# A new written order for the instructions of an attention and expert kernel, from chunk 1 to the end

## The chip, the cores and the metric

The kernel runs on one core of one Trainium2 chip. The core has five engines, each with its own queue of instructions: TensorE (PE, matmuls), VectorE (DVE), ScalarE (ACT), GpSimd (POOL) and SyncE (SP), which here only issues DMAs. The metric is device time in microseconds (us) for one launch.

## The reference

Attention over 8 batches, 8 heads, 576 positions of 64 columns, in two parts that are added: a full attention over q, k and v averaged by fours (144 positions, each result repeated four times), and a local one in which a position sees only those less than four away. The 4608 rows of 512 columns that come out go through a gated layer:

```
q_d = q.reshape(B, H, Sd, 4, D).mean(axis=3)        # k_d, v_d in the same way
out_up = np.repeat(sm_attn(q_d, k_d, v_d), 4, axis=2)
mask = np.abs(pos[:, None] - pos[None, :]) < 4
out_local = softmax(where(mask, scale * q @ k.T, -1e9)) @ v
x = (out_up + out_local).transpose(0, 2, 1, 3).reshape(4608, 512)
out = (np.maximum(x @ w_gate, 0) * (x @ w_val)) @ w_out   # 512 -> 1536 -> 512
```

Inputs and output are float32; matmul operands are fp16.

## The kernel before

**Tiling.** The rows are cut into 9 chunks of 512. The attention of a chunk is done by pairs of heads, four pairs to a chunk, two to each of its two units (`u` 0 and 1; pairs `a` and `b`). While the layer of chunk c is computed, the attention of the next rows and the output product of chunk c-1 are interleaved with it, so that PE always has a matmul.

**Seven products.** The gate layer (`Gate7`, L1295 to L1313: `sq` product, `sk` copy on ACT, `sf` finish on DVE or ACT) and the output layer (`Out7`, the same lines: `up`, `uk`, `uf`) replace eight block products by seven, at the price of fp16 sums of operand blocks. For the output these are sums of the gated activations `gT`, made on DVE by `Unit.sums` (L1030) in four steps of 768 columns, called `sum`, `sumhi` and `next`; the fourth writes the tile `s4`. The sums of x are `xq` (L1282). The value layer (`vh`, L951) is plain, and `gt` (L1390) multiplies gate and value on DVE.

**Attention steps.** `qk` and `v` load from POOL's queue (L468, L486), `v4` loads the v for averaging from SP's queue (L520, two pieces), `scores` computes scores and issues on SP the DMA transpose of q and k three pairs ahead (L529), `pool` averages q and k (L536, DVE), `v2` and `v1` average v by two additions on POOL (L573, L581), `mask` (L862), `xn` and `xsum` (L902, L906) are DVE steps. `after`, `tn` and `tm` are copies of one element on POOL into a tile `seen` (L1465, L1524): they make POOL, and through it whatever depends on POOL's position, wait until a tile has been read or written.

**The order.** Nothing plans the order: it is written out. `SEQ` is one string of 2338 steps, run from first to last under a manual schedule, so each engine gets its instructions in exactly the order in which the steps stand. Semaphore waits are added where data or a buffer demands them. A step such as `sq/4.0.0.1/0@3` says what, with which bank, and for unit 0 of chunk 3; `sq/4.0.2.1/0@3` is the same product with another tile. Steps that begin with `t:` belong to the last two chunks: `q`, `k`, `o` and `qv`, `kv`, `ov` are the layers, `p` (L1199), `s` (L1210) and `e` (L1215, L1217) product, copy and finish of the output, `y` an output DMA of 128 rows by 256 columns on SP. The finished rows lie in `y_sb`, a pool (`ypool`) of four buffers: a later unit's finish into a buffer waits until the DMA that reads it has landed.

The fp16 sums and the guard of `s4`:

```
def sums(self, lo=0, hi=NK, which=range(4)):
    ...
    for o, a, b, op in (ops[i] for i in which):
        nc.vector.tensor_tensor(
            out=o[:, lo:hi, :], in0=a[:, lo:hi, :], in1=b[:, lo:hi, :], op=op
        )
...
"after": lambda w, i: nc.gpsimd.tensor_copy(out=seen, in_=w.s4[:, NK - 1, 127:128]),
...
def emit_v2(hp):
    ...
        nc.gpsimd.tensor_tensor(out=m, in0=t[:, :, 0:128], in1=t[:, :, 128:256], op=ALU.add)
```

Of the kernel before, what the change touches and what calls it, by code (L numbers as in the profile page):

```python
# [42 lines left out]
ex/7/0/4 ma/7/0 hv/9/*/1 hg/9/*/0 relu/9/0 wt/0 hv/10/*/6 hg/10/*/3 relu/10/3 gate/9/1 gate/10/6 qk/a0/1@0
next/0/1@0 vd/7/4 qk/b0/1@0 qk/a1/1@0 hg/11/*/7 relu/11/7 next/1/1@0 flip/9 hv/11/*/0 p/1/0@1 gate/11/0 sumhi/0/0@1
v/a/1@0 vc/7/4 num/7/1/7 tr/8/0/1 keep/1/0@1 zero/b/6 ev/8/01A/1 wt/1 v/b/0@0 num/7/0/6 tr/8/1/0 wt/2 den/7/0/4
den/7/1/5 ln/4 sumhi/1/0@1 p/2/0@1 c11//0@1 zs/1.1/0@1 qk/b2/0@1 qk/b2/1@0 p/6/0@1 vd/8/5 ev/8/00A/1 inv xn/6
p/5/0@1 next/0/0@1 keep/2/0@1 vc/8/5 ev/8/10A/0 p/7/0@1 ev/8/11A/0 scores/a/0@1 exp/a1/0@1 xsum/7 keep/3/0@1
hg/0/0@1 qk/b3/1@0 hv/0/0@1 wt/3 relu/0/0@1 qk/a0/0@1 flip/10 qk/a2/0@1 mask/a1/0@1 hg/2/0@1 next/2/0@1 sum/3/0@1
ed/a/0@1 o/a11/0@1 c22//0@1 exp/a0/0@1 mask/a0/0@1 next/1/0@1 p/4/0@1 o/a01/0@1 qk/a3/0@1 zs/1.0/0@1 tn/1/0@1
gate/0/0@1 c21//0@1 o/a10/0@1 ln/a1/0@1 p/3/0@1 flip/11 next/3/0@1 qk/b3/0@1 c12//0@1 relu/2/0@1 qk/b1/0@1 o/a00/0@1  # L50
ln/a0/0@1 inv/a/0@1 pool/b/0@1 xn/a1/0@1 hg/1/0@1 relu/1/0@1 zero/b/1 v2/a/1@1 hg/4/0@1 zero/b/5 hv/1/0@1 gate/1/0@1
hv/2/0@1 xn/a0/0@1 qk/b0/0@1 vd/9/7 vc/9/7 hg/3/0@1 relu/3/0@1 flip/12 gate/2/0@1 xsum/a/0@1 zs/2.0/0@1 scores/b/0@1
exp/b0/0@1 mask/b0/0@1 exp/b1/0@1 mask/b1/0@1 qk/a3/1@1 hv/3/0@1 gate/3/0@1 vd/10/2 ed/b/0@1 zs/3.0/0@1 vc/10/2
v4/b/1@0 hv/4/0@1 relu/4/0@1 gate/4/0@1 pool/a/0@1 tn/3/0@1 o/b00/0@1 o/b01/0@1 ln/b0/0@1 v/b/1@0 o/b10/0@1
o/b11/0@1 ln/b1/0@1 p/1/1@1 inv/b/0@1 xn/b0/0@1 hg/5/0@1 keep/1/1@1 xn/b1/0@1 hv/5/0@1 p/2/1@1 c11//1@1 p/6/1@1
scores/a/1@1 flip/13 relu/5/0@1 hg/0/1@1 qk/a0/1@1 zero/b/2 p/5/1@1 xsum/b/0@1 qk/a1/1@1 exp/a0/1@1 keep/2/1@1
p/7/1@1 mask/a0/1@1 gate/5/0@1 exp/a1/1@1 mask/a1/1@1 ed/a/1@1 o/a00/1@1 relu/0/1@1 pool/b/1@1 qk/a2/1@1 qk/b0/1@1
keep/3/1@1 c22//1@1 zero/d/0 v/a/0@1 pool/a/1@1 v2/b/0@1 v4/b/0@1 v1/a/1@1 o/a01/1@1 ln/a0/1@1 o/a11/1@1 o/a10/1@1
v/b/0@2 hv/0/1@1 qk/b1/1@1 ln/a1/1@1 inv/a/1@1 const/2 qk/a3/0@2 xn/a0/1@1 p/4/1@1 c21//1@1 p/3/1@1 kk/a0/1@1
kk/a1/1@1 qk/b3/1@1 hg/2/1@1 relu/2/1@1 flip/14 hg/1/1@1 relu/1/1@1 xn/a1/1@1 qk/a1/0@2 scores/b/1@1 exp/b0/1@1  # L60
zero/v/1 qk/a2/0@2 hg/3/1@1 c12//1@1 hv/1/1@1 exp/b1/1@1 gate/0/1@1 qk/a0/0@2 hv/2/1@1 zs/2.1/0@1 zero/b/3 zero/v/0
mask/b1/1@1 tm/b/1@1 v/a/0@2 v4/a/1@1 ed/b/1@1 mask/b0/1@1 o/b00/1@1 o/b10/1@1 zs/3.1/0@1 zero/b/0 gate/1/1@1
zero/d/1 v1/b/1@1 v/a/1@1 o/b01/1@1 relu/3/1@1 ln/b0/1@1 gate/2/1@1 o/b11/1@1 zero/v/2 hv/3/1@1 gate/3/1@1 ln/b1/1@1
qk/b2/1@1 hg/4/1@1 hg/5/1@1 qk/b1/0@2 xsum/a/1@1 inv/b/1@1 xn/b1/1@1 v/b/0@1 xn/b0/1@1 kd/a1/1@1 v2/b/1@1 v4/b/1@1
qk/b0/0@2 hv/4/1@1 kd/a0/1@1 relu/5/1@1 relu/4/1@1 gate/4/1@1 hv/5/1@1 gate/5/1@1 zero/b/4 v/b/1@1 zero/k/1
qk/b3/0@2 qk/b2/0@2 xsum/b/1@1 up/2.1/0@2 xq/0/0@2 xq/1/0@2 kk/b0/0@2 sq/4.0.0.1/0@2 xq/2/0@2 scores/a/0@2
vh/10.6/0@2 uk/2.1/0@2 sk/4.0.0.1/0@2 sq/4.0.0.2/0@2 sq/4.0.0.5/0@2 sq/4.0.0.6/0@2 sumhi/0/0@2 kk/b1/0@2 vh/4.7/0@2
sf/4.0.0.11/0@2 xq/3/0@2 sk/4.0.0.2/0@2 v2/a/0@2 sq/4.0.0.3/0@2 next/0/1@1 sk/4.0.0.5/0@2 sq/4.0.0.7/0@2 up/2.5/0@2
sumhi/1/0@2 exp/a0/0@2 ed/a/0@2 next/1/1@1 kk/a1/0@2 sf/4.0.0.22/0@2 sq/4.0.0.4/0@2 sf/4.0.0.21/0@2 mask/a0/0@2
sf/4.0.0.12/0@2 gt/4.7.0/0@2 up/2.6/0@2 uk/2.2/0@2 uk/2.5/0@2 sq/0.0.2.1/0@2 sq/0.0.2.5/0@2 sk/0.0.2.5/0@2 sum/2/0@2  # L70
sum/3/0@2 gt/10.6.1/0@2 o/a00/0@2 o/a01/0@2 up/2.7/0@2 sk/0.0.2.1/0@2 uf/2.22/0@2 sq/0.0.2.6/0@2 sk/0.0.2.2/0@2
ln/a0/0@2 inv/a/0@2 pool/b/0@2 next/0/0@2 up/2.2/0@2 o/a10/0@2 sq/0.0.2.3/0@2 sq/0.0.2.2/0@2 sf/0.0.2.11/0@2
sq/0.0.2.7/0@2 v1/a/0@2 after/3/0@2 sf/0.0.2.22/0@2 sf/0.0.2.12/0@2 kd/b0/0@2 o/a11/0@2 xn/a0/0@2 up/2.4/0@2
kd/b1/0@2 up/2.3/0@2 uf/2.21/0@2 v2/b/0@2 uf/2.11/0@2 uf/2.12/0@2 sq/0.0.2.4/0@2 sf/0.0.2.21/0@2 pool/a/0@2
sq/1.1.0.1/0@2 sq/1.1.0.5/0@2 sk/1.1.0.5/0@2 scores/b/0@2 v4/b/0@2 vh/0.7/0@2 sk/1.1.0.1/0@2 sq/1.1.0.6/0@2 v1/b/0@2
exp/b0/0@2 gt/0.7.2/0@2 vh/6.3/0@2 gt/6.3.3/0@2 mask/b0/0@2 sk/1.1.0.2/0@2 kd/a0/0@2 sq/1.1.0.2/0@2 sq/1.1.0.7/0@2
sf/1.1.0.22/0@2 ed/b/0@2 kd/a1/0@2 sq/1.1.0.3/0@2 kk/a0/0@2 v4/a/0@2 vh/1.0/0@2 o/b00/0@2 sf/1.1.0.11/0@2 kk/b1/1@2
sq/1.1.0.4/0@2 sf/1.1.0.21/0@2 o/b01/0@2 sf/1.1.0.12/0@2 ln/b0/0@2 o/b10/0@2 sq/2.2.0.1/1@2 sq/2.2.0.5/1@2
vh/7.1/0@2 o/b11/0@2 xsum/a/0@2 sk/2.2.0.1/1@2 next/2/0@2 sq/2.2.0.6/1@2 sq/2.2.0.2/1@2 inv/b/0@2 scores/a/1@2
sk/2.2.0.5/1@2 gt/1.0.0/0@2 qk/a1/1@2 gt/7.1.1/0@2 xn/b0/0@2 sk/2.2.0.2/1@2 v1/a/1@2 up/0.1/1@2 tm/b/0@2 qk/b3/1@2  # L80
sq/2.2.0.7/1@2 v/a/1@2 ed/a/1@2 sq/2.2.0.3/1@2 sf/2.2.0.11/1@2 kk/a0/1@2 up/0.5/1@2 sf/2.2.0.22/1@2 sq/2.2.0.4/1@2
sf/2.2.0.21/1@2 next/1/0@2 v2/b/1@2 uk/0.1/1@2 sf/2.2.0.12/1@2 qk/a0/1@2 qk/a2/1@2 vh/8.7/1@2 pool/b/1@2 qk/a1/0@3
sq/3.2.1.1/1@2 up/0.6/1@2 gt/8.7.1/1@2 exp/a0/1@2 mask/a0/1@2 kd/b0/1@2 sq/3.2.1.5/1@2 vh/2.4/1@2 gt/2.4.0/1@2
sk/3.2.1.1/1@2 sq/3.2.1.2/1@2 sk/3.2.1.5/1@2 sq/3.2.1.6/1@2 uk/0.2/1@2 uk/0.5/1@2 qk/a3/1@2 xsum/b/0@2 o/a00/1@2
o/a11/1@2 sk/3.2.1.2/1@2 next/3/0@2 tm/a/1@2 up/0.7/1@2 uf/0.22/1@2 sf/3.2.1.11/1@2 o/a01/1@2 v/b/1@2 sq/3.2.1.3/1@2
sq/3.2.1.7/1@2 o/a10/1@2 sf/3.2.1.22/1@2 kk/b0/1@2 pool/a/1@2 kd/b1/1@2 ln/a0/1@2 sf/3.2.1.12/1@2 up/0.2/1@2
inv/a/1@2 xn/a0/1@2 sq/3.2.1.4/1@2 sf/3.2.1.21/1@2 scores/b/1@2 v/b/0@3 exp/b0/1@2 up/0.3/1@2 sq/5.2.0.1/1@2
ed/b/1@2 sq/5.2.0.5/1@2 sk/5.2.0.5/1@2 up/0.4/1@2 mask/b0/1@2 o/b00/1@2 xsum/a/1@2 sk/5.2.0.1/1@2 sq/5.2.0.6/1@2
uf/0.21/1@2 uf/0.11/1@2 uf/0.12/1@2 o/b01/1@2 vh/3.0/1@2 gt/3.0.1/1@2 tm/b/1@2 vh/9.1/1@2 gt/9.1.2/1@2
sk/5.2.0.2/1@2 v2/a/1@2 o/b10/1@2 sq/5.2.0.7/1@2 qk/b1/1@2 qk/b2/1@2 v1/b/1@2 qk/a0/0@3 sq/5.2.0.3/1@2 ln/b0/1@2  # L90
sq/5.2.0.2/1@2 o/b11/1@2 sf/5.2.0.22/1@2 qk/a2/0@3 vh/5.4/1@2 inv/b/1@2 v4/b/1@2 kd/a0/1@2 qk/b0/1@2 qk/b3/0@3
sf/5.2.0.12/1@2 xn/b0/1@2 qk/a3/0@3 sf/5.2.0.11/1@2 sq/5.2.0.4/1@2 qk/b0/0@3 v4/a/1@2 qk/b2/0@3 v/a/0@3
sf/5.2.0.21/1@2 gt/5.4.0/1@2 xsum/b/1@2 vh/11.1/1@2 gt/11.1.1/1@2 kk/a1/1@2 kd/a1/1@2 qk/b1/0@3 up/2.1/0@3 xq/0/0@3
xq/1/0@3 kk/b0/0@3 sq/4.0.0.1/0@3 xq/2/0@3 scores/a/0@3 vh/10.6/0@3 uk/2.1/0@3 sk/4.0.0.1/0@3 sq/4.0.0.2/0@3
sq/4.0.0.5/0@3 sq/4.0.0.6/0@3 sumhi/0/0@3 kk/b1/0@3 vh/4.7/0@3 sf/4.0.0.11/0@3 xq/3/0@3 sk/4.0.0.2/0@3 v2/a/0@3
sq/4.0.0.3/0@3 next/0/1@2 sk/4.0.0.5/0@3 sq/4.0.0.7/0@3 up/2.5/0@3 sumhi/1/0@3 exp/a0/0@3 ed/a/0@3 next/1/1@2
kk/a1/0@3 sf/4.0.0.22/0@3 sq/4.0.0.4/0@3 sf/4.0.0.21/0@3 mask/a0/0@3 sf/4.0.0.12/0@3 gt/4.7.0/0@3 up/2.6/0@3
# [1526 lines left out]
```

## Time and profile before

| what | value |
|---|---|
| time, median of 3 runs | 343.49 us (342.92 to 344.7) |
| the profiled execution | 343.54 us, span 341.8 us |
| clock granted to TensorE | 1.00 in every stretch |
| PE busy | 331.0 us, 97% of the span |
| DVE, ACT, POOL busy | 292.9, 272.1, 188.6 us |
| transfers | 43.91 MB, 128 GB/s in the mean |

The page gives for each engine its busy time, share and instructions; for a group of instructions its line, engine, operation, output and inputs, shapes, count, then busy time and the mean in ns; in square brackets or behind a bar the idle time just before and what ended it. A row of the timeline begins with its start and its length in us. A DMA row ends with the KB of one and the median us from issue to landing. The span is the recorded stretch; the execution's own time is 1.7 us longer. In the steady part, chunks 2 to 5, one chunk takes about 35 us.

### The profile page before, as it was taken

How to read it: one execution, taken by the hardware profiler on the slowest of the kernel's cores; microseconds unless marked ns; L12 is line 12 of the kernel's file. 1: busy time of each engine (PE TensorE's matmuls, PEld its weight loads, DVE VectorE, ACT ScalarE, POOL GpSimd, SP SyncE). 2: the span in 40 equal slices, each digit the busy share in tenths (PEclk: the TensorE clock that was granted, in tenths of full speed). 3: DMA queues.
4: the chain of work that ended last, by engine and by line, in shares of the span. 5: the costliest groups of instructions: out<-in, count | busy, mean ns of one | idle time of the engine just before them, and what ended most of it. 6: DMA issues, size and time to landing. Idle time of an engine off the chain costs nothing.

```text
span 341.8 us, 9062 instructions
## 1 busy us (share of the span) xinstructions
PE 331.0 (97%) x3410; PEld 243.5 (71%) x3410; DVE 292.9 (86%) x578; ACT 272.1 (80%) x653; POOL 188.6 (55%) x268
## 2 busy tenths in 40 slices
...
GB/s 135 165 170 208 185 194 167 150 186 148 168 187 133 192 88 218 128 185 105 220 118 194 92 191 151 189 122 190 51 33 1 63 2 93 3 15 109 3 56 130
DMA packets 162176, 43.91 MB, mean 128 GB/s; under 512 B 147500, under 2 KB 156820, under 8 KB 162132
## 3 DMA queue, kind: packets, MB, share of 16 engines
...
q10 hardware_dynamic: 112, 0.02, 0.0%
...
## 4 chain that ended last, share of the span: by engine, by line
PE 79%; DMA 6%; DVE 5%; POOL 4%; ACT 3%; issue 2%; DVEq 0%; ACTq 0%; POOLq 0%
PE ps L1295 24%; PE ps L951 24%; PE ps L1199 17%; DMA qk<-in_k_dram 3%; PE ps L1036 3%; DMA wv_sb<-in_moe_w_val_dram 3%; PE ps L867 2%; POOL qk L463 2%; PE ps L840 2%; PE ps L887 1%; PE ps L882 1%; POOL vw L513 1%; PE ps L836 1%; DVE xo L1030 1%; DVE xT L1175 1%
## 5 line engine op out<-in xcount | busy, mean ns | idle before, releaser
L951 PE MATMUL ps<-xT,wv_sb 128*128 128x512 f16 x352 | 89.4, 379 | 0.0
L951 PEld LDWEIGHTS <-wv_sb 128*128 128x128 f16 x352 | 32.5, 97 | 27.5
L468 POOL DMA_DIRECT2D qk<-in_k_dram x46 | 33.6, 732 | 19.3 <-DMA qkT<-qk 16.3
L1390 DVE SCALAR_TENSOR_TENSOR gT<-r,ps 128x512 f16<-128x512 f16 x55 | 37.5, 682 | 6.1 <-PE ps L951 5.1
L1295 PE MATMUL ps<-xT,qk 128*128 128x256 f16 x240 | 40.9, 272 | 0.0
L468 POOL DMA_DIRECT2D qk<-in_q_dram x46 | 34.0, 740 | 12.1 <-DMA qkT<-qk 7.1
L1306 ACT COPY ps<-ps 128x256 f32<-128x256 f32 x80 | 29.0, 366 | 8.1 <-PE ps L1295 7.4
L1295 PE MATMUL ps<-xT,wg_sb 128*128 128x256 f16 x180 | 33.9, 272 | 1.1 <-DVE xT L1313 0.6
L536 DVE TENSOR_REDUCE qkd<-qkT 128x288 f16<-128x1152 f16 x23 | 30.8, 1338 | 0.0
L486 POOL DMA_DIRECT2D vw<-in_v_dram x40 | 28.9, 732 | 2.3 <-DMA qk<-in_q_dram 1.7
L1311 ACT CAST r<-ps 128x256 f16<-128x256 f32 x55 | 20.2, 367 | 11.0 <-DVE r L1313 6.3
L581 POOL TENSOR_TENSOR vd<-v 48x192 f16<-48x192 f32 x40 | 26.0, 650 | 1.7
L1210 ACT COPY ps<-ps 128x256 f32<-128x256 f32 x54 | 19.4, 366 | 9.1 <-PE ps L1199 7.3
L951 PE MATMUL ps<-xT,wg_sb 128*128 128x512 f16 x104 | 26.1, 380 | 0.5 <-ACT r L960 0.5
L1295 PEld LDWEIGHTS <-qk 128*128 128x128 f16 x240 | 22.2, 97 | 4.8
L573 POOL TENSOR_TENSOR v<-v 112x384 f32<-112x384 f32 (+1 forms) x21 | 22.6, 1074 | 4.0 <-DMA v<-in_v_dram 3.6
L1295 PEld LDWEIGHTS <-xo 128*128 128x128 f16 x240 | 22.5, 97 | 2.9 <-DVE xo L1030 0.2
L1295 PEld LDWEIGHTS <-wg_sb 128*128 128x128 f16 x180 | 17.0, 97 | 10.7 <-issue 3.1
L1295 PE MATMUL ps<-wt,xo 128*128 128x256 f16 x180 | 24.5, 272 | 0.0
L920 ACT ACTIVATE rden<-rden 128x720 f32<-128x720 f32 x28 | 22.5, 803 | 0.8
L1313 DVE TENSOR_TENSOR r<-ps,xT 128x256 f16<-128x256 f32 x44 | 18.1, 418 | 4.4 <-PE ps L1295 3.1
L963 DVE TENSOR_TENSOR gT<-r,ps 128x512 f16<-128x512 f16 x24 | 16.1, 679 | 6.0 <-PE ps L951 3.2
...
## 6 DMA issues: line engine op xcount, KB each, us to landing
...
v<-in_v_dram SPq DMA_DIRECT2D x20, 192.0 KB, 5.1
...
v<-in_v_dram SPq DMA_DIRECT2D x20, 144.0 KB, 5.2
...
```

Of the source, the lines that this page charges most:

```text
L468: nc.gpsimd.dma_start(dst.rearrange("p (j h d) -> p j h d", h=2, d=64)[:, :, hh, :], _dap(src, off + hh * S * D, [[D, 96], [NQ * D, NB], [ ...
L486: nc.gpsimd.dma_start(t[lo : lo + 64, j0:j1, lo : lo + 64], _dap(v, base + j0 * QB * D, [[D, 64], [QB * D, j1 - j0], [1, D]]),)
L536: nc.vector.tensor_reduce(out=qkd[hp % 2].rearrange("p i t -> p (i t)"), in_=qkT[hp % 4][:, 0 : 2 * S].rearrange("p (t f) -> p t f", f=4), ...
L573: nc.gpsimd.tensor_tensor(out=m, in0=t[:, :, 0:128], in1=t[:, :, 128:256], op=ALU.add)
L581: nc.gpsimd.tensor_tensor(out=vp[hp % 3][lo : lo + 48, :, lo : lo + 64], in0=m[:, :, 0:64], in1=m[:, :, 64:128], op=ALU.add)
L920: nc.scalar.activation(out=rden, in_=rden, func=AF.Exp, scale=-1.0)
L951: nc.tensor.matmul(out=out, lhsT=w[:, kk, bass.ts(jj, 128)], rhs=xT[:, kk, c * TCH : (c + 1) * TCH], start=(kk == 0), stop=(kk == 3),)
L1199: nc.tensor.matmul(out=out, lhsT=self.left[i][t], rhs=self.right[i][t], start=(i == 1 and t == 0), stop=(t == n - 1), skip_group_check=True,)
L1295: nc.tensor.matmul(out=out, lhsT=self.left[i - 1][k], rhs=self.right[i - 1][k], start=(i == 1 and k == 0), stop=(k == n - 1), skip_group_c ...
L1306: nc.scalar.copy(out=o, in_=x)
L1311: nc.scalar.copy(out=o, in_=self.d if i == 11 else self.a)
L1390: lambda c, jj, b, t: nc.vector.scalar_tensor_tensor(out=gT[c % 2][:, jj, :], in0=tg[t], scalar=0.0, in1=ps[:, b, :], op0=ALU.max, op1=ALU ...
```

## The change

Only `SEQ` differs, in some 215 lines. Its first 273 steps stay as they are (to about 45 us of the trace); from there to the end the same steps stand in another order, on every engine. No step is added or removed, and each engine has as many instructions as before. Of the steps, 387 name another PSUM bank or gate tile (`sq/4.0.0` becomes `sq/4.0.2`, `vh/10.6` becomes `vh/10.4`). Chunks 2 to 5 have one pattern each, in both orders.

What moves, where the prediction speaks of it: the additions `v1` and `v2` of a chunk stand in other places of POOL's queue; `after/3/0`, which stood between `v1/a/0` and `v2/b/0`, stands directly behind `v2/b/1`, and `next/3/0` on DVE directly behind it; in the last two chunks `y/7/1/0/0` stands behind `y/8/0/0/1` instead of before the last layer's matmuls, and the finishes and output DMAs of chunk 8 stand in another order. A step of a pair of heads that does not exist, such as `qk/a0/0@7`, issues nothing.

The diff, cut to the first unit of chunk 3 and the end (line numbers of the new file are one higher below `SEQ`):

```diff
--- before
+++ after
...
-o/a01/0@3 up/2.7/0@3 sk/0.0.2.1/0@3 uf/2.22/0@3 sq/0.0.2.6/0@3 sk/0.0.2.2/0@3 ln/a0/0@3 inv/a/0@3 pool/b/0@3
-next/0/0@3 up/2.2/0@3 o/a10/0@3 sq/0.0.2.3/0@3 sq/0.0.2.2/0@3 sf/0.0.2.11/0@3 sq/0.0.2.7/0@3 v1/a/0@3 after/3/0@3
-sf/0.0.2.22/0@3 sf/0.0.2.12/0@3 kd/b0/0@3 o/a11/0@3 xn/a0/0@3 up/2.4/0@3 kd/b1/0@3 up/2.3/0@3 uf/2.21/0@3 v2/b/0@3
-uf/2.11/0@3 uf/2.12/0@3 sq/0.0.2.4/0@3 sf/0.0.2.21/0@3 pool/a/0@3 sq/1.1.0.1/0@3 sq/1.1.0.5/0@3 sk/1.1.0.5/0@3
-scores/b/0@3 v4/b/0@3 vh/0.7/0@3 sk/1.1.0.1/0@3 sq/1.1.0.6/0@3 v1/b/0@3 exp/b0/0@3 gt/0.7.2/0@3 vh/6.3/0@3
-gt/6.3.3/0@3 mask/b0/0@3 sk/1.1.0.2/0@3 kd/a0/0@3 sq/1.1.0.2/0@3 sq/1.1.0.7/0@3 sf/1.1.0.22/0@3 ed/b/0@3 kd/a1/0@3
-sq/1.1.0.3/0@3 kk/a0/0@3 v4/a/0@3 vh/1.0/0@3 o/b00/0@3 sf/1.1.0.11/0@3 kk/b1/1@3 sq/1.1.0.4/0@3 sf/1.1.0.21/0@3
...
-sk/2.2.0.1/1@3 next/2/0@3 sq/2.2.0.6/1@3 sq/2.2.0.2/1@3 inv/b/0@3 scores/a/1@3 sk/2.2.0.5/1@3 gt/1.0.0/0@3 qk/a1/1@3
-gt/7.1.1/0@3 xn/b0/0@3 sk/2.2.0.2/1@3 v1/a/1@3 up/0.1/1@3 tm/b/0@3 qk/b3/1@3 sq/2.2.0.7/1@3 v/a/1@3 ed/a/1@3
-sq/2.2.0.3/1@3 sf/2.2.0.11/1@3 kk/a0/1@3 up/0.5/1@3 sf/2.2.0.22/1@3 sq/2.2.0.4/1@3 sf/2.2.0.21/1@3 next/1/0@3
-v2/b/1@3 uk/0.1/1@3 sf/2.2.0.12/1@3 qk/a0/1@3 qk/a2/1@3 vh/8.7/1@3 pool/b/1@3 qk/a1/0@4 sq/3.2.1.1/1@3 up/0.6/1@3
-gt/8.7.1/1@3 exp/a0/1@3 mask/a0/1@3 kd/b0/1@3 sq/3.2.1.5/1@3 vh/2.4/1@3 gt/2.4.0/1@3 sk/3.2.1.1/1@3 sq/3.2.1.2/1@3
-sk/3.2.1.5/1@3 sq/3.2.1.6/1@3 uk/0.2/1@3 uk/0.5/1@3 qk/a3/1@3 xsum/b/0@3 o/a00/1@3 o/a11/1@3 sk/3.2.1.2/1@3
-next/3/0@3 tm/a/1@3 up/0.7/1@3 uf/0.22/1@3 sf/3.2.1.11/1@3 o/a01/1@3 v/b/1@3 sq/3.2.1.3/1@3 sq/3.2.1.7/1@3 o/a10/1@3
...
-t:ov/8/4/12 t:p/7/1/4 t:ov/8/4/21 t:gatev/8/4/0 t:o/8/4/21 t:hv/8/5/0 t:e/7/1/11 t:gatev/8/4/1 t:e/7/1/21
-t:y/7/1/0/0 t:hv/8/5/1 t:y/7/1/1/1 t:gate/8/5/0 t:sum/8/0/0/0/5 t:p/8/1/1 t:gate/8/5/1 t:p/8/0/1 t:sum/8/0/0/5/6
-t:sum/8/1/0/0/6 t:p/8/0/5 t:e/7/1/12 t:sum/8/0/1/0/5 t:p/8/1/5 t:y/7/1/0/1 t:sum/8/0/1/5/6 t:s/8/0/1 t:sum/8/1/2/0/6
-t:y/7/1/1/0 t:s/8/0/5 t:p/8/0/2 t:sum/8/1/1/0/6 t:s/8/1/1 t:s/8/1/5 t:sum/8/0/3/0/6 t:p/8/0/6 t:sum/8/0/2/0/6
-t:p/8/1/6 t:sum/8/1/3/0/6 t:s/8/0/2 t:p/8/1/2 t:p/8/0/3 t:s/8/1/2 t:p/8/1/7 t:e/8/0/11 t:p/8/0/7 t:y/8/0/0/0
-t:e/8/0/12 t:e/8/1/22 t:y/8/0/0/1 t:p/8/1/3 t:e/8/0/22 t:y/8/1/1/1 t:p/8/0/4 t:y/8/0/1/1 t:e/8/1/11 t:e/8/1/12
-t:y/8/1/0/0 t:p/8/1/4 t:e/8/0/21 t:y/8/1/0/1 t:e/8/1/21 t:y/8/0/1/0 t:y/8/1/1/0
...
+kk/a0/1@2 qk/b0/0@3 qk/b3/0@3 v/b/0@3 xq/0/0@3 v1/a/0@3 up/2.1/0@3 scores/a/0@3 uk/2.1/0@3 v2/b/0@3 sq/4.0.2.1/0@3
+sumhi/0/0@3 exp/a0/0@3 xq/1/0@3 next/0/1@2 xq/3/0@3 sumhi/1/0@3 vh/4.6/0@3 sk/4.0.2.1/0@3 up/2.2/0@3 ed/a/0@3
+kk/b1/0@3 sq/4.0.2.5/0@3 sq/4.0.2.6/0@3 xq/2/0@3 vh/10.4/0@3 v2/a/0@3 sk/4.0.2.2/0@3 sk/4.0.2.5/0@3 sum/2/0@3
+kk/b0/0@3 next/1/1@2 sq/4.0.2.3/0@3 sq/4.0.2.7/0@3 kk/a0/0@3 sf/4.0.2.22/0@3 mask/a0/0@3 sq/4.0.2.2/0@3 up/2.5/0@3
+sq/4.0.2.4/0@3 sf/4.0.2.21/0@3 sf/4.0.2.12/0@3 sum/3/0@3 sf/4.0.2.11/0@3 gt/10.4.3/0@3 up/2.6/0@3 uk/2.2/0@3
+pool/b/0@3 gt/4.6.2/0@3 uk/2.5/0@3 sq/0.0.1.1/0@3 sq/0.0.1.5/0@3 sk/0.0.1.5/0@3 sk/0.0.1.1/0@3 o/a00/0@3 o/a01/0@3
+ln/a0/0@3 up/2.3/0@3 sq/0.0.1.6/0@3 sk/0.0.1.2/0@3 up/2.7/0@3 uf/2.22/0@3 o/a11/0@3 kd/b0/0@3 sq/0.0.1.7/0@3
+sf/0.0.1.22/0@3 kd/b1/0@3 sq/0.0.1.3/0@3 sf/0.0.1.12/0@3 v1/a/1@3 v1/b/0@3 o/a10/0@3 inv/a/0@3 xn/a0/0@3
...
+sq/1.0.0.1/0@3 sq/1.0.0.5/0@3 vh/6.6/0@3 gt/6.6.2/0@3 sk/1.0.0.1/0@3 sq/1.0.0.6/0@3 uf/2.11/0@3 uf/2.12/0@3
+sq/1.0.0.2/0@3 vh/0.2/0@3 ed/b/0@3 exp/b0/0@3 v4/b/0@3 o/b00/0@3 sk/1.0.0.5/0@3 sk/1.0.0.2/0@3 mask/b0/0@3
+gt/0.2.1/0@3 sq/1.0.0.3/0@3 sq/1.0.0.7/0@3 sf/1.0.0.22/0@3 o/b01/0@3 kk/a1/0@3 sf/1.0.0.12/0@3 kd/a1/0@3 ln/b0/0@3
+next/2/0@3 vh/1.3/0@3 kd/a0/0@3 next/0/0@3 sf/1.0.0.11/0@3 sq/1.0.0.4/0@3 sf/1.0.0.21/0@3 gt/1.3.0/0@3
+sq/2.2.0.1/1@3 next/1/0@3 v4/a/0@3 sq/2.2.0.5/1@3 sk/2.2.0.5/1@3 scores/a/1@3 pool/b/1@3 vh/7.1/0@3 sk/2.2.0.1/1@3
+qk/a1/1@3 o/b11/0@3 ed/a/1@3 gt/7.1.1/0@3 inv/b/0@3 sq/2.2.0.6/1@3 up/0.1/1@3 up/0.5/1@3 qk/a0/1@3 sk/2.2.0.2/1@3
+sq/2.2.0.3/1@3 sq/2.2.0.7/1@3 exp/a0/1@3 qk/a3/1@3 vh/8.5/1@3 sf/2.2.0.12/1@3 o/b10/0@3 v2/b/1@3 kk/b1/1@3
+sf/2.2.0.22/1@3 sq/2.2.0.4/1@3 uk/0.1/1@3 after/3/0@3 next/3/0@3 sf/2.2.0.21/1@3 sq/2.2.0.2/1@3 sf/2.2.0.11/1@3
+xsum/a/0@3 mask/a0/1@3 up/0.6/1@3 tm/b/0@3 tm/a/1@3 gt/8.5.1/1@3 kd/b1/1@3 uk/0.2/1@3 v/a/1@3 sq/3.2.1.1/1@3
+sk/3.2.1.1/1@3 vh/2.4/1@3 xn/b0/0@3 qk/a2/1@3 sq/3.2.1.6/1@3 sq/3.2.1.2/1@3 qk/a1/0@4 qk/b0/1@3 sq/3.2.1.5/1@3
...
+t:qv/8/4/4 t:ov/8/4/21 t:gatev/8/4/0 t:o/8/4/21 t:gatev/8/4/1 t:p/7/1/4 t:hv/8/5/0 t:e/7/1/21 t:y/7/1/1/0 t:o/8/5/11
+t:gate/8/5/0 t:sum/8/0/0/0/5 t:hv/8/5/1 t:gate/8/5/1 t:sum/8/1/0/0/6 t:p/8/1/1 t:sum/8/0/0/5/6 t:p/8/0/1 t:p/8/0/5
+t:e/7/1/12 t:sum/8/0/1/5/6 t:s/8/0/1 t:y/7/0/1/0 t:p/8/1/5 t:y/7/1/0/1 t:sum/8/0/1/0/5 t:sum/8/1/2/0/6 t:p/8/0/2
+t:s/8/0/5 t:s/8/1/1 t:s/8/1/5 t:sum/8/1/1/0/6 t:sum/8/1/3/0/6 t:p/8/0/6 t:p/8/1/6 t:p/8/1/2 t:s/8/0/2
+t:sum/8/0/3/0/6 t:p/8/0/3 t:sum/8/0/2/0/6 t:p/8/0/7 t:y/7/0/1/1 t:e/8/0/22 t:y/8/0/1/1 qk/a0/0@7 t:e/8/0/12
+t:y/8/0/0/1 t:s/8/1/2 t:p/8/1/7 t:e/8/1/22 t:p/8/1/3 t:e/8/1/12 t:p/8/0/4 v4/b/1@6 t:y/7/1/0/0 t:y/8/1/1/1
+t:e/8/1/11 t:y/8/1/0/0 t:p/8/1/4 t:e/8/1/21 t:e/8/0/11 t:e/8/0/21 t:y/8/0/1/0 qk/b3/1@6 qk/b2/0@7 t:y/8/1/1/0
+t:y/8/1/0/1 kd/a1/1@6 t:y/8/0/0/0
```

384 lines of the change are left out of this document (190 added, 194 removed).

## Prediction

> **What bounds the kernel now.** I read the page first (engines, chain), then the groups by form, then the timeline around PE's late starts, the transfers, and the last twelve microseconds.
>
> ```profile
> PE 331.0 (97%) x3410; PEld 243.5 (71%) x3410; DVE 292.9 (86%) x578; ACT 272.1 (80%) x653; POOL 188.6 (55%) x268
> PE 79%; DMA 6%; DVE 5%; POOL 4%; ACT 3%; issue 2%; DVEq 0%; ACTq 0%; POOLq 0%
> ```
>
> PE is the bound, and the change leaves its 3410 matmuls alone. An order can save only the time by which PE starts late. Busy time hides that, because a matmul counts as busy until its modelled end, so I went by starts. From the chain of waits near the end:
>
> ```profile
> 278.56 48.69 PE ps L1199 x444
> 329.93 8.33 PE ps L1199 x76
> ```
>
> That is 8.33 / 76 = 0.110 us from one 128x256 matmul to the next, 0.66 us for a product of six, with nothing late. A row that starts later than this after its forerunner shows a late start. Over 85 to 280 us such delays sum to 10.7 us, of which 7.0 us lie in delays above 70 ns; the rest is scattered. So about 7 us, 2% of the time, is the most that a reordering can win there.
>
> Where they come from is seen in the timeline near 178 us:
>
> ```profile
> 174.35 0.55 DVE L1030 TENSOR_TENSOR xo<-gT,xo 128x768 f16<-128x768 f16 x1
> ...
> 177.17 1.00 POOL L573 TENSOR_TENSOR v<-v 112x384 f32<-112x384 f32 x1
> 177.19 1.39 DVE L1030 TENSOR_TENSOR xo<-gT 128x768 f16<-128x768 f16 x1
> 177.79 0.82 PE L1295 MATMUL ps<-wo_sb,xo 128*128 128x256 f16 x6
> 178.13 1.56 POOL L581 TENSOR_TENSOR vd<-v 48x192 f16<-48x192 f32 x2
> 178.51 0.41 DVE L1313 TENSOR_TENSOR xT<-ps,xT 128x256 f16<-128x256 f32 x1
> 178.97 0.71 PE L1295 MATMUL ps<-xT,wg_sb 128*128 128x256 f16 x4 [0.36 <-DVE xT L1313]
> ```
>
> One fp16 sum of 768 columns takes 0.55 us, another 1.39 us, begun 20 ns after an addition of pooled v on POOL that runs until 178.17. The next finish on DVE (L1313) comes late, and PE starts 178.97 - 177.79 = 1.18 us after a product that needs 0.66: 0.52 us lost. The groups by form give the mean over the kernel: the first row's sums fall in the stretch where POOL adds pooled v, the second's after it.
>
> ```profile
> L1030 DVE TENSOR_TENSOR xo<-gT 128x768 f16<-128x768 f16 x18 | 12.2, 678 | 0.0
> L1030 DVE TENSOR_TENSOR vw<-gT 128x768 f16<-128x768 f16 x9 | 4.9, 549 | 0.0
> ```
>
> **The gains, part by part.** (a) Chunks 2 to 6. The same wait of PE recurs at 102.3, 137.22, 172.39, 207.56 and 242.13 us, so three periods measure 35.17, 35.17 and 34.57 us. The delays above 70 ns in the second are 1.01 us (0.39 of it from a held sum), in the third 1.00 us (0.52), in the fourth 0.36, which puts the period without them at 34.2 in all three: the estimates agree. In the new order, with the old durations laid on it, five v additions (`v1/a/0`, `v2/b/0`, `v2/a/0`, `v1/a/1`, `v1/b/0`) run after `sum/3/0` and before `next/2/0`, next to reductions, normalizations and gate products. Their rows do not vary (the reduction of L536 has 1.34 us each time), so no sum is held. The three other causes, a finish just ahead of the product that needs its bank (0.10, 0.16, 0.11 us), are apart too: the new banks `4.0.2`, `1.0.0`, `0.0.1` let products start sooner. Saved: 1.0 us each in chunks 2, 3 and 4, 0.36 in 5, 0.5 in 6 (0.08 + 0.17 + 0.17 + 0.11): 3.9 us.
>
> (b) 45 to 100 us. Delays of 2.3 us lie there; the largest (0.63, 0.53, 0.54) end with a relu or copy on ACT behind a full queue of DVE. The new order shortens DVE's lag by some 0.4 us and frees one of the three: 0.9 us.
>
> (c) 276 us. PE waits for a sum of chunk 7's first unit, queued behind two weight sums of 0.95 us:
>
> ```profile
> 276.10 0.71 PE L1199 MATMUL ps<-wt,vw 128*128 128x256 f16 x5
> 276.81 0.42 DVE L1184 TENSOR_TENSOR xT<-xT 128x512 f16<-128x512 f16 x1
> 277.14 0.22 DVE L1030 TENSOR_TENSOR vw<-gT 128x128 f16<-128x128 f16 x1
> 277.42 0.28 PE L1199 MATMUL ps<-wt,vw 128*128 128x256 f16 x1 [0.61 <-DVE vw L1030]
> ```
>
> 1.32 us between starts for five matmuls (0.55): 0.78 us, which go, since the small sum now stands earlier. Next late there is nothing that I find.
>
> Together 5.6 us; bounds 3.0 (only (a) for chunks 2 to 4) and 7.8 (all delays of 85 to 280 us and 0.8 of the rest).
>
> **The price on POOL and DVE.** `after/3/0` is a one-element copy on POOL behind which unit 0's `s4` may be written anew by `next/3/0` on DVE. Before, it stands between two v additions of the start of the chunk (177.03) and the sum follows at 193.36, 16 us later. Now it stands behind `v2/b/1`, which waits for the two SP loads `v4/b/0`, which SP issues behind the output DMA `uf/2.12/0`, some 7.2 us ahead of the point where the sum is due. Laid out by durations, `next/3/0` starts 1.0 us after the second piece lands plus an addition's 1.0 us, with DVE idle ahead of it 0.5 to 0.8 us. Behind it on DVE stand `xsum/a`, `mask/a0`, the gate product `gt/8.5.1`, `xn/b0`, `gt/2.4.0`, and the matmuls `o/a01` of PE need a bank that the last of these frees. With a landing of 5.5 us they come 0.29 us late; at 5.2 us not at all. What the landing will be, the trace brackets:
>
> ```profile
> v<-in_v_dram SPq DMA_DIRECT2D x2, 192.0 KB, 3.7
> v<-in_v_dram SPq DMA_DIRECT2D x2, 144.0 KB, 3.5
> ...
> v<-in_v_dram SPq DMA_DIRECT2D x2, 192.0 KB, 6.3
> v<-in_v_dram SPq DMA_DIRECT2D x2, 144.0 KB, 6.5
> ```
>
> The first pair is issued at 182.6 to 185.4 us, with one load of POOL in flight, the second at 164.2 to 166.6, with eight. For the very load, four chunks give 3.2, 5.4, 3.3 and 4.0 us for the second piece. In the new order three loads of POOL and one output are in flight beside it, nearer to the first. I take 5.2 on average with a scatter on both sides, 0.25 us per chunk over chunks 2 to 5: 1.0 us. Bounds: 0 (3.7) and 1.5 per chunk (6.7): 6 us. A POOL that waits there delays `qk/a2/1`, `v/a/1` and `qk/a1/0` behind it by the same; their transposes have 3.7 us in hand. The transposes and loads otherwise come in another order with the same count, and POOL at 55% hides their issues.
>
> For the small ones I cannot see (a finish a bit late, a bank taken too soon) I put 0.3 us, bounds -0.5 and 2.
>
> **The price at the end.** Of the last two chunks' outputs, `y/7/1/0/0` is issued at 327.6 now, 10 us ahead of the last product's start. In the new order SP issues it only after `y/8/0/0/1`, and `e/8/1/12` writes the same buffer of the four of `ypool`, so it waits for that DMA to land. Let X be the end of the last product (338.24 before):
>
> ```profile
> 334.99 0.37 ACT L1217 COPY y_sb<-ps 128x256 f32<-128x256 f32 x1 [0.30 <-PE ps L1199]
> 335.38 4.09 SPq L986 DMA_DIRECT2D out_dram<-y_sb  x8
> ...
> 338.28 0.37 ACT L1217 COPY y_sb<-ps 128x256 f32<-128x256 f32 x1 [0.28 <-PE ps L1199]
> ```
>
> Eight issues in 4.09 us, in a run about 0.45 each; the last starts at 339.07 = X + 0.83, and the span ends 2.7 us later. After: `p/8/0/7` is four products from the end, X - 2.62; `e/8/0/22` and `e/8/0/12` end at X - 1.8; SP issues `y/8/0/1/1`, `y/8/0/0/1`, `y/7/1/0/0`, the last at X - 1.2. The page has 1.8 us to landing for 128 KB: X + 0.6. Then `e/8/1/12` (0.42) to X + 1.0, and on ACT, queued behind it in order, `e/8/1/11`, `e/8/1/21`, `e/8/0/11`, `e/8/0/21` (0.37, then 0.27 each) to X + 2.2. Four more issues follow on SP, the last at X + 3.6. That is 2.8 us later than now. Bounds: 1.5, if the landing cost nothing (three issues still stand behind the last copy), and 4.8 with the 3.8 us of the page's larger output. No cover is left there: PE has ended.
>
> **The sum.** The profiled run took 343.54 us (span 341.8), the median of the three runs is 343.49, so they may be used for one another. 343.5 - 5.6 + 1.0 + 0.3 + 2.8 = 342.0. Since gains of a rearranged queue arrive in part more often than whole, I take off 0.5 us of them: 342.5.
>
> **Rivals.** *The pooled v load decides (slower).* If the landing of `v4/b/0` is 6.2 us or more, each of chunks 2 to 5 loses 1.0 us, all that it gained: 343.5 - 1.6 + 0.3 + 2.8 = 345, up to 347 at 6.7. For it: DMA 6% in the chain, 6.3 to 6.5 in the sister load. Against it: 3.2 to 5.4 for this load itself. It decides from 5.8 us on. Chance 0.22.
>
> *The gains don't come* because the queues only wait elsewhere: 343.5 - 1 + 0.3 + 2.8 = 345.6. For it: DVE at 86% has few gaps; the fourth period shows that 34.6 is reached where little is held, which speaks against. Chance 0.10.
>
> *The end costs less, or the gains are whole:* 343.5 - 6.3 + 0.3 + 2.0 = 339.5 to 341.5. Chance 0.16.
>
> *The additions hold their new neighbours too.* One normalized sum (L765) lies wholly beside POOL's additions:
>
> ```profile
> 92.75 1.74 POOL L581 TENSOR_TENSOR vd<-v 48x192 f16<-48x192 f32 x2
> 93.28 0.75 DVE L765 TENSOR_TENSOR xT<-xn 128x576 f16<-128x576 f16 x1
> ```
>
> 0.75 us, its usual time (749 ns over eight). If instead these were held as the sums are, by 0.85 us once a chunk, four chunks would come to 3.4 us less gain: 345.9. Chance 0.02. The Trainium skill, GPSIMD Engine Reference (Specifications), speaks for this one: it puts contention on DVE instructions in a 2-port mode or with two SBUF inputs, and this sum has two. The row disagrees, though it is one.
>
> **How the numbers follow.** The forecast has 0.50, within 341.2 to 343.8. What a measurement here can tell from no change is about 0.5%, 1.7 us, so faster means under 341.8. Of the forecast 0.19 lie there and 0.31 between; the cheap end adds 0.16 to faster. Of the load's rival 0.06 stay between; its other 0.16, the gains that don't come and the held neighbours are slower: 0.28. The range leaves out the best of the cheap end and the worst of the load: 340.3 to 346.4.
>
> **What would show it.** Right: sums of L1030 near 550 ns in mean; periods near 34.3 us; no late start at 276; DVE idle ahead of `next/3/0` until POOL; the last output issue some 3.5 us after PE's end, ACT idle before its last copies until DVE, DVE until a DMA. Wrong: landings of v over 5.8 us, PE late at `o/a01`, or an end as short as before.

## The result, and the profile after

The changed order is slower: 346.14 us median of 20 runs (343.71 to 347.6) against 344.32 for before, also of 20 runs (342.92 to 346.41). The ratio is 1.0056, 95% interval 1.0037 to 1.0075: 1.9 us. Forecast was 342.5, "the same", with 343.5 for before from its first three runs. The profiled execution took 346.89 us, its span is 344.9. The engines and the chain on its page:

```profile
PE 330.6 (96%) x3410; PEld 243.6 (71%) x3410; DVE 294.7 (85%) x578; ACT 270.7 (78%) x653; POOL 186.5 (54%) x268
PE 57%; DMA 18%; POOL 10%; DVE 8%; issue 4%; ACT 1%; SPq 1%; ACTq 0%; POOLq 0%; DVEq 0%
```

PE does the same work, 330.6 against 331.0 us. DVE is busier by 1.8 us with the same 578 instructions, so some of them became longer, which is the contrary of what keeping the additions away from sums should give. DMA and POOL were 6% and 4% of the chain and are 18% and 10%.

The starts of the same matmuls in both traces show where the time went. PE begins chunk 2 (`up/2.1/0@2`) at 98.26 instead of 96.39 us: 1.9 lost. From there to the last product (337.53 against 337.43) it gains 1.8. The last output issue of SP ends 4.2 us after PE's last matmul instead of 1.2: 3.0 lost, and this is nearly the whole 3.1 us by which the span grew.

**The sums and their neighbours.** From the groups by form of the changed kernel:

```profile
L907 DVE TENSOR_TENSOR xT<-xn 128x576 f16<-128x576 f16 x20 | 16.0, 800 | 0.1
L649 DVE TENSOR_TENSOR att<-att,cst_sb 112x576 f16<-112x576 f16 x24 | 13.0, 560 | 1.9 <-ACT att L643 1.8
L1031 DVE TENSOR_TENSOR xo<-gT 128x768 f16<-128x768 f16 x18 | 9.9, 569 | 0.0
```

Before has for the first two:

```profile
L906 DVE TENSOR_TENSOR xT<-xn 128x576 f16<-128x576 f16 x20 | 15.0, 751 | 0.0
L648 DVE TENSOR_TENSOR att<-att,cst_sb 112x576 f16<-112x576 f16 x24 | 10.2, 450 | 1.8 <-ACT att L642 1.8
```

The sums that had a mean of 678 ns are down to 569. That part of the change does what it says. But the 24 masks of the first pairs (L649) rose from 450 to 560 ns in the mean, all of it in three masks of chunk 1 (2.06, 1.06 and 0.83 us), and `xsum` (L907) from 751 to 800, in two rows of 1.15 and 1.33 us. The timeline of chunk 1:

```profile
72.73 2.06 DVE L649 TENSOR_TENSOR att<-att,cst_sb 112x576 f16<-112x576 f16 x1
73.44 1.04 POOL L574 TENSOR_TENSOR v<-v 112x384 f32<-112x384 f32 x1
74.86 0.30 PE L780 MATMUL ps<-att,vw 112*128 112x96 f16 x3 [0.80 <-DVE att L649]
...
81.24 1.80 DVE L1031 TENSOR_TENSOR xo<-gT,xo 128x768 f16<-128x768 f16 x1
81.43 1.19 POOL L574 TENSOR_TENSOR v<-v 72x512 f32<-72x512 f16 x1
83.43 0.81 PE L1037 MATMUL ps<-wt,xo 128*128 128x256 f16 x6 [0.93 <-DVE y_sb L1074]
```

A mask of 0.45 us takes 2.06, a sum of 0.55 takes 1.80, and behind each PE sits idle for 0.8 to 0.9 us. The sum lies beside an addition for all but its first 0.19 us. The mask begins 0.71 us ahead of the addition's record, while POOL issues two loads of v (until 73.36 us); the last section comes back to this.

**The wait for the pooled v.** Chunk 3, the same view:

```profile
154.09 1.00 POOL L574 TENSOR_TENSOR v<-v 112x384 f32<-112x384 f32 x1 [6.29 <-DMA v<-in_v_dram]
155.03 0.19 POOL L1466 COPY seen<-xo 128x1 f16<-128x1 f16 x1
155.25 0.56 DVE L1031 TENSOR_TENSOR xo<-gT,xo 128x768 f16<-128x768 f16 x1 [1.66 <-POOL seen L1466]
158.18 0.68 DVE L1391 SCALAR_TENSOR_TENSOR gT<-r,ps 128x512 f16<-128x512 f16 x1
158.91 0.28 PE L883 MATMUL ps<-att,one_st 128*128 128x290 f16 x1 [0.25 <-DVE gT L1391]
```

This is the chain of the prediction: load, addition, guard (the copy into `seen`), `next/3/0`, and at its end `gt/2.4.0` and the matmul `o/a01`. The second pieces of v landed after 5.1, 6.2, 5.4 and 5.1 us in chunks 2 to 5, and PE was late by 0.21, 1.28, 0.41 and 0.41 us by its starts.

**The end.** The last stretch in the chain of waits, and the timeline beside it:

```profile
337.14 1.84 DMA out_dram<-y_sb
```

```profile
336.27 6.29 SPq L987 DMA_DIRECT2D out_dram<-y_sb  x9
336.87 1.47 PE L1200 MATMUL ps<-xT,gT 128*128 128x256 f16 x12
339.05 0.42 DVE L1216 TENSOR_TENSOR y_sb<-ps,vw 128x256 f32<-128x256 f32 x1 [2.15 <-DMA out_dram<-y_sb]
339.51 1.20 ACT L1218 COPY y_sb<-ps 128x256 f32<-128x256 f32 x4 [4.70 <-DVE y_sb L1216]
```

`y/7/1/0/0` is issued at 337.14 and takes 1.84 us to land; DVE waits for it, ACT's four copies wait for DVE, and SP's issues trail to 342.56.

### The profile page after: what moved, and what is told of

Read it like the earlier page. It is cut to its first block, busy times and chain, and to the rows that moved or that the text cites. A ratio compares the mean times of both kernels' runs of the same rounds, so it can differ in the third digit from the quotient of the medians.

```text
span 344.9 us, 9106 instructions
## 1 busy us (share of the span) xinstructions
PE 330.6 (96%) x3410; PEld 243.6 (71%) x3410; DVE 294.7 (85%) x578; ACT 270.7 (78%) x653; POOL 186.5 (54%) x268
## 4 chain that ended last, share of the span: by engine, by line
PE 57%; DMA 18%; POOL 10%; DVE 8%; issue 4%; ACT 1%; SPq 1%; ACTq 0%; POOLq 0%; DVEq 0%
PE ps L1296 20%; PE ps L1200 17%; PE ps L952 13%; DMA v<-in_v_dram 5%; DMA wo_sb<-in_moe_w_out_dram 4%; DMA vw<-in_v_dram 4%; DMA wg_sb<-in_moe_w_gate_dram 3%; POOL qk L469 3%; POOL qk L464 3%; POOL vw L514 2%; DVE gT L1391 2%; PE ps L868 2%; PE ps L883 1%; DMA qk<-in_q_dram 1%; PE ps L888 1%
## 5 line engine op out<-in xcount | busy, mean ns | idle before, releaser
L952 PE MATMUL ps<-xT,wv_sb 128*128 128x512 f16 x352 | 90.4, 379 | 0.0
L574 POOL TENSOR_TENSOR v<-v 112x384 f32<-112x384 f32 (+1 forms) x21 | 21.1, 1013 | 20.8 <-DMA v<-in_v_dram 20.3
L1296 PE MATMUL ps<-xT,wg_sb 128*128 128x256 f16 x180 | 31.7, 272 | 0.0
L582 POOL TENSOR_TENSOR vd<-v 48x192 f16<-48x192 f32 x40 | 24.3, 607 | 1.9
L1312 ACT CAST r<-ps 128x256 f16<-128x256 f32 x55 | 19.2, 374 | 7.2 <-PE ps L1296 5.9
L1296 PEld LDWEIGHTS <-gT 128*128 128x128 f16 x180 | 17.2, 98 | 3.9
```

Of the source, the lines that this page charges most:

```text
L582: nc.gpsimd.tensor_tensor(out=vp[hp % 3][lo : lo + 48, :, lo : lo + 64], in0=m[:, :, 0:64], in1=m[:, :, 64:128], op=ALU.add)
L952: nc.tensor.matmul(out=out, lhsT=w[:, kk, bass.ts(jj, 128)], rhs=xT[:, kk, c * TCH : (c + 1) * TCH], start=(kk == 0), stop=(kk == 3),)
L1296: nc.tensor.matmul(out=out, lhsT=self.left[i - 1][k], rhs=self.right[i - 1][k], start=(i == 1 and k == 0), stop=(k == n - 1), skip_group_c ...
```

## The experiments

Theory after the result: three separate losses, the end (3 us), the wait for the pooled v (2.3 us) and the additions in chunk 1 (1 to 2 us), against a gain of about 4 us in chunks 2 to 6 and at 276 us. Rival: the order is a net in which what one wait frees the next takes. All medians, with the ratio to before from the same chip:

| run | edit | median us | ratio to before, 95% |
|---|---|---|---|
| changed kernel | | 346.14 | 1.0056 (1.0037 to 1.0075) |
| a_y | `y/7/1/0/0` early | 344.88 | 1.0010 (0.9978 to 1.0043) |
| a_end | end as before | 342.74 | 0.9941 (0.9916 to 0.9966) |
| a_guard | `after/3/0` early | 344.62 | 0.9994 (0.9969 to 1.0019) |
| a_sep | the same, `v2/b/1` later | 343.82 | 0.9993 (0.9971 to 1.0014) |
| ba | chunk 1 as before | 345.17 | 1.0016 (0.9991 to 1.0040) |
| ab | only chunk 1 changed | 344.90 | 1.0020 (0.9994 to 1.0047) |
| b_y | before, `y/7/1/0/0` late | 344.33 | 1.0009 (0.9988 to 1.0030) |
| a_small | small additions | 342.15 | 0.9940 (0.9913 to 0.9968) |
| b_small | before, small additions | 341.42 | 0.9926 (0.9899 to 0.9953) |
| best | ba, a_guard and a_end | 340.66 | 0.9898 (0.9869 to 0.9926) |
| best2 | ba, a_sep and a_end | 340.53 | 0.9891 (0.9867 to 0.9915) |

Before itself had medians of 344.1 to 344.4 in these groups of runs. Single executions of one kernel lie up to 3 us from their median, so one profile shows a mechanism and not a size to a tenth. A difference of two medians is good to about 1 us either way: drawing the runs again puts the 1.3 us of `a_y` between 0.1 and 2.3, and the 3.4 us of `a_end` between 2.9 and 4.3.

In the diffs below the lines of `SEQ` are cut to the steps around each move. The line numbers in these runs' profiles are 6 or 7 lower than in the kernel that was edited.

**The output DMA at the end.**

```diff
-t:y/7/1/1/0 t:o/8/5/11
+t:y/7/1/1/0 t:y/7/1/0/0 t:o/8/5/11
...
-t:e/8/1/12 t:p/8/0/4 v4/b/1@6 t:y/7/1/0/0 t:y/8/1/1/1
+t:e/8/1/12 t:p/8/0/4 v4/b/1@6 t:y/8/1/1/1
```

> The changed kernel with one step moved: the output DMA y/7/1/0/0 is issued right behind y/7/1/1/0, before the last products, instead of behind y/8/0/0/1. Theory (the end is set by the landing of this DMA, for which e/8/1/12 waits): e/8/1/12 follows p/8/1/3 at once, and the last issue of SP comes 2.3 to 2.4 us after the last product's end instead of 3.8, since three more issues still stand behind the last copy; 1.4 us less than the changed kernel. Rival (SP's string of issues sets the end whatever the landing does): no change of the end, within 0.3 us.

1.3 us less by the medians. In its trace the last issue ends 2.9 us after PE, against 4.2. The landing is worth 1.3. Four issues in a row still follow the last copy (341.26 to 343.05 us): its own and the three of the forecast.

> The changed kernel with the finishes, sums and output DMAs from the product p/8/1/2 on in the order of before, and y/7/1/0/0 and y/7/0/1/1 issued ahead of them. Theory: last issue 0.8 us after the last product's end as before, 3.0 us less than the changed kernel, so about level with before (the rest of the order is worth nothing: PE reached its last product at 337.53 against 337.43). Rival (the later end comes from PE or from slower landings of the outputs): less than 1 us.

3.4 us less by the medians, and the last issue ends 1.0 us after PE. The edit sorts the steps from `p/8/1/2` on as before has them. So the end is the largest loss, 1.3 of it the landing and 2.1 the order of finishes and issues. The expectation that the remaining order is worth nothing was too low: the kernel is now 0.6% under before.

> Before with one step moved: y/7/1/0/0 is issued behind y/8/0/0/1, as in the changed kernel. Theory: e/8/0/22 writes the same buffer and waits for its landing (issue at 336.3, 1.8 us), the outputs behind it on SP follow at 0.45 us each, last issue at 340.4 instead of 339.1: 1.3 us more than before. Rival (a DMA of 128 KB in the end is hidden): within 0.3 us of before.

A miss: 0.3 us by the medians, not measurable. It is not `e/8/0/22` that waits but `e/8/1/11` on ACT, and not for `y/7/1/0/0`. The chain of waits, and the timeline beside it:

```profile
336.46 1.76 DMA out_dram<-y_sb
```

```profile
338.38 1.12 ACT L1211 COPY y_sb<-ps 128x256 f32<-128x256 f32 x3 [2.40 <-DMA out_dram<-y_sb]
338.78 0.42 DVE L1209 TENSOR_TENSOR y_sb<-ps,vw 128x256 f32<-128x256 f32 x1 [1.44 <-ACT y_sb L1211]
```

The DMA issued at 336.46 is the second in SP's string of nine, `y/8/0/0/1`; `y/7/1/0/0` is the third, at 336.87. In this order `e/8/1/11` took the buffer that `y/8/0/0/1` reads, and no later finish reuses that of `y/7/1/0/0`. The product before it had ended at 337.54, so 0.8 us of the landing of `y/8/0/0/1` is uncovered, and the last issue ends 1.7 us after PE, 0.5 later than before. So `b_y` does not price the landing of `y/7/1/0/0`; `a_y` does. In the changed kernel that landing itself is waited for, with four copies and five issues queued behind it.

**The guard of s4.**

```diff
-qk/a1/1@3 o/b11/0@3
+after/3/0@3 qk/a1/1@3 o/b11/0@3
...
-sf/2.2.0.22/1@3 sq/2.2.0.4/1@3 uk/0.1/1@3 after/3/0@3 next/3/0@3
+sf/2.2.0.22/1@3 sq/2.2.0.4/1@3 uk/0.1/1@3 next/3/0@3
```

> The changed kernel with after/3/0 of chunks 2 to 5 moved on POOL from behind v2/b/1 to ahead of the load qk/a1/1, so that next/3/0 on DVE no longer waits for the pooled v to land. Theory: the late starts at o/a01 of 0.21, 1.28, 0.41 and 0.41 us go; 2.3 us less. Rival (DVE's queue is late there anyway, or POOL waiting behind v2/b/1 delays the loads): 0 to 0.5 us less, with late starts at the same matmuls.

1.5 us less by the medians. `next/3/0` no longer idles for POOL, but a new thing appears. Its trace in chunk 4:

```profile
188.47 0.55 DVE L1025 TENSOR_TENSOR xo<-gT,xo 128x768 f16<-128x768 f16 x1
188.75 1.13 POOL L568 TENSOR_TENSOR v<-v 112x384 f32<-112x384 f32 x1 [5.48 <-DMA v<-in_v_dram]
188.94 1.55 DVE L901 TENSOR_TENSOR xT<-xn 128x576 f16<-128x576 f16 x1
192.93 0.41 PE L877 MATMUL ps<-att,one_st 128*128 128x290 f16 x2 [0.16 <-DVE gT L1385]
```

The guard behind `v2/b/1` had also kept DVE idle while the addition ran. Without it, `xsum/a` (usually 0.75 us) runs beside the addition and takes 1.55; in chunk 3 it is the mask behind it that takes 1.25. In both chunks `o/a01` is late by 0.32 us. `a_sep` adds a second move:

```diff
-o/b10/0@3 v2/b/1@3 kk/b1/1@3
+o/b10/0@3 kk/b1/1@3
...
-tm/b/0@3 tm/a/1@3 gt/8.5.1/1@3
+tm/b/0@3 tm/a/1@3 v2/b/1@3 gt/8.5.1/1@3
```

> The changed kernel with after/3/0 of chunks 2 to 5 ahead of qk/a1/1, as in the run before, and v2/b/1 behind tm/a/1, that is, beside a gate product and xn instead of beside xsum/a and mask/a0. Theory: moving the guard alone gave 1.5 of 2.3 us because v2/b/1 then held xsum or a mask (1.56 and 1.25 us in two chunks, PE still 0.32 late); with both moved no late start is left at o/a01 of chunks 2 to 5: 2.3 us less than the changed kernel. Rival (the guard moved alone gave all there is): 1.5 us less, or 0 if v2/b/1 later delays the load v4/b/1.

2.3 us less by the medians, as expected, and its trace has no late start at `o/a01` of chunks 2 to 5:

```profile
187.45 0.75 DVE L900 TENSOR_TENSOR xT<-xn 128x576 f16<-128x576 f16 x1
188.12 0.45 DVE L856 TENSOR_TENSOR att<-att,zero_sb 128x576 f16<-128x576 f16 x1
188.83 1.00 POOL L567 TENSOR_TENSOR v<-v 112x384 f32<-112x384 f32 x1
189.08 0.90 DVE L896 TENSOR_TENSOR xn<-ps,rden 128x720 f16<-128x720 f32 x1
```

The ratios to before of the two runs are alike (0.9994 and 0.9993), so the traces show the difference between them, the times do not settle it.

**Chunk 1.** `SEQ` is cut where both orders have done the same steps, at `up/2.1/0@2`; `ba` takes the start from before, `ab` from the changed kernel.

> Order of before up to the start of chunk 2 (its first product up/2.1), order of the changed kernel from there on. Theory: the changed order is worse in chunk 1, where masks and an fp16 sum of 0.45 to 0.55 us lie beside POOL's additions and take 2.07, 1.80, 1.06 and 0.84 us: 1.9 us less than the changed kernel, PE at chunk 2 at 96.4 us. Rival (the start of chunk 1 is shifted by landings of loads, which differ from run to run): within 0.5 us of the changed kernel.

> Order of the changed kernel up to the start of chunk 2, order of before from there on: the changed chunk 1 alone. Theory: 1.0 to 2.0 us more than before, with a mask and next/3/0 of 1.5 to 2.1 us beside the additions v2/a/1 and v2/b/0 and PE at chunk 2 at 98.3 instead of 96.4. Rival (the loss of chunk 1 belongs to the way its new order meets the new chunk 2): within 0.5 us of before.

`ba` is 1.0 us faster than the changed kernel, `ab` 0.5 us slower than before by the medians (the interval of its ratio includes no change). Both have the expected sign and half the expected size. In the traces it is plainer: PE begins chunk 2 at 96.0 with before's start and at 97.8 with the changed one. The other traces agree: six with before's start begin chunk 2 at 96.0 to 97.2, six with the changed one at 97.4 to 100.4. The loss is there, 0.5 to 1.0 us at the end; where the rest of the 1.9 us is regained is not shown.

**What the additions cost.**

```diff
-nc.gpsimd.tensor_tensor(out=m, in0=t[:, :, 0:128], in1=t[:, :, 128:256], op=ALU.add)
+n = 2 if hp >= NEW else 128
+nc.gpsimd.tensor_tensor(out=m[:, :, 0:n], in0=t[:, :, 0:n], in1=t[:, :, 128 : 128 + n], op=ALU.add)
...
-out=vp[hp % 3][lo : lo + 48, :, lo : lo + 64], in0=m[:, :, 0:64], in1=m[:, :, 64:128], op=ALU.add
+out=vp[hp % 3][lo : lo + 48, :, lo : lo + 2], in0=m[:, :, 0:2], in1=m[:, :, 0:2], op=ALU.add
```

> Before with the additions of pooled v cut to 2 columns of 128 and 64 for all pairs of chunks 1 on (the rest of the sums is left out), so that they hardly run beside DVE. Theory: no sum, mask or xq is held any more (4 us of DVE time in all), and the late starts that come from them go (0.5 at 98 us, 0.4 at 105, 0.4 at 143, 0.5 at 178): 1.8 us less than before. Rival (DVE has room, held sums are hidden): less than 0.5 us.

> The changed kernel with the same cut additions. Theory: the late starts in chunk 1 (0.97, 1.10, 0.34, 0.36, 0.50, behind held masks and a held sum) go but for some 1 us, next/3/0 starts 0.9 us sooner since v2/b/1 is short (1.9 us less at o/a01), and 0.6 us at the start of chunk 6 goes: 4.5 us less than the changed kernel. Rival (what costs in the changed kernel are the loads and the order itself, not the additions): less than 2 us.

Both kernels leave out most of the sums of v. They do not cut the additions of one pair in chunk 1 (`v2/b/0` with 1.2 us, `v1/a/1`): beside these `next/3/0` still takes 2.00 us in `a_small` and `mask/a0` 1.05.

2.7 us less than before and 4.0 us less than the changed kernel: the other additions cost each order that much, as neighbours of DVE and as time in POOL's queue. In `a_small`, which has the changed start, PE begins chunk 2 at 96.4 and `mask/b1` takes its usual 0.45 us, so the loss of chunk 1 goes with the additions. Of the 4.0, up to 1.9 are `v2/b/1` as a link in the wait for s4. That leaves an estimate of 4.0 - 1.9 = 2.1 us or more for the contention with DVE in the changed kernel, hardly less than before's 2.7. In the traces it has moved from sums to masks and `xsum`, and into chunk 1.

> Before, and behind its end seven forms of DVE instruction in turn, three times each alone, three times beside a string of 26 additions of pooled v on POOL (the output is the same, the extra time says nothing). Theory: an instruction that reads two SBUF tensors is held by an addition that began first, by up to the 1.0 us of the addition: fp16 sum 0.55 to 1.0 or more, mask 0.45 and difference of x 0.42 likewise, xsum 0.75 to 1.1 or more; the reduction (1.34), the gate product (0.68) and xn (0.90), which read one SBUF tensor, as alone. Twice each beside a string of loads issued by POOL: as alone, but for a rare one. Rival (my reading before: xsum isn't held): xsum stays at 0.75 beside additions; second rival (loads hold as much as additions): sums of 0.9 us and more in the last part.

The timeline of the appended forms, alone (sum, xsum, difference of x, reduction, gate product, xn, mask):

```profile
347.45 0.55 DVE L1024 TENSOR_TENSOR vw<-gT 128x768 f16<-128x768 f16 x1
347.92 0.75 DVE L900 TENSOR_TENSOR xT<-xn 128x576 f16<-128x576 f16 x1
348.59 0.41 DVE L1178 TENSOR_TENSOR xT<-xT 128x512 f16<-128x512 f16 x1
348.92 1.34 DVE L530 TENSOR_REDUCE qkd<-qkT 128x288 f16<-128x1152 f16 x1
350.19 0.67 DVE L1399 SCALAR_TENSOR_TENSOR gT<-r,ps 128x512 f16<-128x512 f16 x1
350.78 0.90 DVE L896 TENSOR_TENSOR xn<-ps,rden 128x720 f16<-128x720 f32 x1
351.60 0.45 DVE L856 TENSOR_TENSOR att<-att,zero_sb 128x576 f16<-128x576 f16 x1
...
364.06 1.34 DVE L1024 TENSOR_TENSOR vw<-gT 128x768 f16<-128x768 f16 x1
365.32 1.54 DVE L900 TENSOR_TENSOR xT<-xn 128x576 f16<-128x576 f16 x1
366.79 1.21 DVE L1178 TENSOR_TENSOR xT<-xT 128x512 f16<-128x512 f16 x1
367.92 1.34 DVE L530 TENSOR_REDUCE qkd<-qkT 128x288 f16<-128x1152 f16 x1
369.18 0.67 DVE L1399 SCALAR_TENSOR_TENSOR gT<-r,ps 128x512 f16<-128x512 f16 x1
369.78 0.89 DVE L896 TENSOR_TENSOR xn<-ps,rden 128x720 f16<-128x720 f32 x1
370.59 0.71 DVE L856 TENSOR_TENSOR att<-att,zero_sb 128x576 f16<-128x576 f16 x1
```

Beside a string of additions sum, `xsum` and difference of x take 0.79 to 0.80 us longer, a mask 0.26 to 0.40; reduction, gate product and xn nothing. All of the held ones read two tensors from SBUF, the gate product and xn one from SBUF and one from PSUM, the reduction one. The additions pay less: their rows last 0.99 to 1.39 us, 1.08 in the mean, against a median of 1.00 in the same kernel. Beside loads of q and k issued by POOL all forms have their usual time, in the one round that fell there. This is the rule that the Trainium skill, GPSIMD Engine Reference (Specifications), gives, contention for an instruction with two SBUF inputs, and here the rule is borne out.

**All three undone.**

> Order of before up to the start of chunk 2, the changed order from there with after/3/0 of chunks 2 to 5 ahead of qk/a1/1, and from p/8/1/2 on the finishes and outputs in the order of before. Theory (three separate losses: end 3.4, guard 1.5, chunk 1 1.0 us by the medians of the three runs that undo one each): they add, 346.1 - 5.9 = 340.2 us, 1.2% under before. Rival (they share a cover, what one frees the next gives back): 342 us or more.

> The version of before's chunk 1, the changed chunks 2 to 6 and before's end, now with v2/b/1 behind tm/a/1 too. Theory: 0.5 to 0.8 us less than with the guard alone (340.7): 340.0 us. Rival: no less than 340.7.

340.66 us, 1.0% under before: 5.5 us less than the changed kernel where 5.9 were forecast, so the losses add, nearly. The rival of a net in which gains are given back falls. With `v2/b/1` moved as well it is 340.53: no gain on top that could be measured, a miss against the expected 0.5 to 0.8. Its profile has masks of 0.78 to 0.86 us beside `v1/b/0`, and one late start of 0.35 us behind such a mask, at 147.1; the additions again found other neighbours. Both beat before and the changed kernel.

## Why the prediction was wrong

The text put -5.6, +1.0, +0.3 and +2.8 together, then took 0.5 off the gains. By the runs the terms are:

- *Gains (a) and (c), 4.7 us (chunks 2 to 6, and the sum at 276), 4.2 with the 0.5 taken off.* Right. `best2` is before's chunk 1 and end with the changed middle freed of the wait: 3.9 us under before. In `a_sep`, where the wait is gone too, PE goes from chunk to chunk in 34.26, 34.19 and 34.18 us where before needs 35.16, 35.17 and 34.57: the 34.2 of the prediction. The late start of 0.78 at 276 is gone.
- *Gain (b), 0.9 us at 45 to 100 us.* Wrong in sign: 0.5 to 1.0 us lost. This is the step that failed, and the largest part of the miss, some 1.7 us. The new order was laid out with the usual durations of DVE, and for chunk 1 I never asked which additions stand beside which masks and sums. `v2/a/1`, `v2/b/0` and `v1/a/1` stand beside `mask/b1`, `next/3/0` and `mask/a0`, which take 2.06, 1.80 and 1.06 us instead of 0.45, 0.55 and 0.45. For `mask/b1` a share of the loads of v is not excluded.
- *The wait for the pooled v, 1.0 us (0 to 6).* The mechanism was right to the instruction, the term too small: about 1.5 to 2.3. Landings of the second piece came to 5.1 to 6.2 us, 5.45 in the mean, not 5.2. And the break-even was set too high: two landings of 5.1 us, which the prediction has on time at 5.2, were late by 0.2 and 0.4. In all four chunks `o/a01` starts 5.0 us after the landing, and the load is issued 9.6 to 10.0 us before it is due, which leaves 4.7 to 5.0 us for the landing. So all four came late, by 0.2 to 1.3.
- *The end, 2.8 us (1.5 to 4.8).* Right in every link; 3.0 in the trace, 3.4 by the medians. The bound of 1.5 for a landing without cost is the 2.1 that `a_y` leaves.
- *The neighbours that aren't held (chance 0.02).* Wrong in its reason. One row, an `xsum` of 0.75 us beside an addition, was taken as proof. In that row the two additions took 1.74 us instead of their usual 1.2, so there it was POOL that was held; in the string of additions `xsum` takes 1.54. In the changed kernel two `xsum` of 1.15 and 1.33 us near 233 and 238 us make PE 0.6 us late at the start of chunk 6. The Trainium skill, GPSIMD Engine Reference (Specifications), which spoke for this rival, was right against my row.

With these, 344.3 - 3.9 + 0.8 + 1.9 + 3.4 = 346.5, near the measured 346.1; the 0.3 put for small ones has no run of its own. The rival that came nearest is "the gains don't come" at 345.6, but its reason (the queues wait elsewhere) isn't what happened: most gains came and three prices were higher than put.
